# Loading batch 0 pair by pair, starting its products at unit 5, and turning its last 64 tokens in one group

## The chip, the cores and the metric

The kernel runs on one core of a Trainium2 chip. A core has five engines that run their own instruction streams side by side and wait for each other through semaphores: TensorE (matrix multiplications into PSUM), VectorE and ScalarE (elementwise work, evacuation of PSUM), GpSimd (here copies, and the issue of all loads that cast from fp32 to fp16) and SyncE (issue of stores and of transposes by DMA). Sixteen DMA engines move the data. The metric is the device time of one execution in microseconds, less is better.

## The reference: attention, then a gated feed-forward network

```python
# q, k, v: (8 batches, 12 heads, 448 tokens, 64), fp32
scores = (q @ k.transpose(0, 1, 3, 2)) / sqrt(64)
attn   = softmax(scores, axis=-1)
x      = (attn @ v).transpose(0, 2, 1, 3).reshape(8 * 448, 768)
# w_gate, w_val: (768, 1536), w_out: (1536, 768)
g   = x @ w_gate
out = (g * sigmoid(g) * (x @ w_val)) @ w_out      # (3584, 768), fp32
```

## The kernel before

Two heads make a pair; 6 pairs make a batch, 48 pairs in all. The 448 tokens of a head are taken as 4 chunks of 112. A unit is one chunk of keys of one pair: scores of both heads (two matmuls), one exponential on ScalarE over 112 x 896, and one piece of the product with the values (8 matmuls, summed in PSUM over the 4 chunks of the pair). Units 0 to 23 are batch 0; only after them does the feed-forward network have an input, X, which is kept transposed (features on partitions, two batches of tokens side by side in one tile). Blocks of feed-forward work alternate between 384 and 512 tokens: block 0 is tokens 0 to 383 of batch 0, block 1 is the rest of batch 0 and all of batch 1.

Queries and keys are turned by TensorE for pairs 0 to 10 and by DMA from pair 11 (`NPE`) on. The product of a pair, divided by its sums, is turned into X by TensorE for pairs 0 to 11 and by DMA from pair 12 (`XPE`) on.

```python
NPE = 11; LA = 6; RB = 5; FIRST = 6; WIDE = 8; XPE = 12
NE = 4; NX = 3; NV = 6; VS = 6      # buffers of E, xt, vo, and pairs in vraw

def load_qk16(pr, n=2):             # n pairs of q and of k, cast by the load
    ...
        nc.gpsimd.dma_start(dst[:, ds(h0, 2 * n)], flat...)

def load_v(pr, n=1):                # n pairs of values
    ...
def copy_v(pr):
    nc.vector.tensor_copy(Vts[pr % NV][:, :, :, 0:D], vraw[:, pr % VS])

    def turn():                     # in prep(pr): q and k of one pair
        ...
        for t in range(2):
            for c in range(NC):
                for hx in range(2):
                    src = raw[pr][t][:, hx, c, :]
                    nc.tensor.transpose(tp[ts(hx, 64), (1 - t) * NC + c, 0:P], src, ident[0:P, 0:P])
        nc.vector.tensor_copy(qkT[pr][:, 0 : 2 * S]..., tp[:, :, 0:P])
        nc.vector.tensor_copy(qkT[pr][:, 2 * S :], tp[:, NC, 0:D])

def qk(pr, c):                      # one unit: scores and exponential
    ...
    nc.scalar.activation(e[:, :, 0:S], s[0:P, :, 0:S], AF.Exp, scale=sm_scale)

def pv_chunk(pr, c):                # one piece; after the last one:
    ...
    nc.vector.reciprocal(r[:, 0:7], a7[:, :, D])
    nc.vector.tensor_tensor(xt..., a7[:, 0:n, 0:D], r..., ALU.mult)

def turn_x(pr):                     # into X: 3 x 128 tokens and a rest of 64
    ...
    if pr < XPE:
        for j in range(3):
            nc.tensor.matmul(tp[:, ds(D + 128 * j, 128)], lhsT=xt[:, j], rhs=ident[:], ...)
        for hx in range(2):
            nc.tensor.matmul(tp[ts(hx, D), 0:D], lhsT=xt[:, 3, 0:D], rhs=ident[:, ts(hx, D)], ...)
        nc.vector.tensor_copy(dst, tp[:, 0:S])
        return
    nc.sync.dma_start_transpose(dst[:, D:S]..., xt[:, 0:3]...)
    nc.sync.dma_start_transpose(dst[:, 0:D]..., xt[0:D, 3])

# ---- order of work at the start ----
load_qk32(0)                        # pair 0 in fp32, from SyncE
load_qk16(1, 1); load_qk16(2, 1); load_qk16(3, 1)
load_v(0, GP)                       # pairs 0 to 2 (GP = 3) in one transfer
load_qk16(4)                        # pairs 4 and 5
load_v(3, GP)
...
wq = {                              # more loads, when a pair is entered
    0: [("qk", 6), ("g", 0), ("v", 0)],
    1: [("qk", 8), ("g", 1), ("v", 1)],
    3: [("qk", 10), ("V", 2), ("g", 2), ("v", 2)],
    4: [("g", 3), ("v", 3), ("qk", 12)],
    6: [("V", 3), ("o", 0)],        # w_out, in two halves
    7: [("o", 1)],
}
for u in range(FIRST * NC):         # batch 0
    pr, c = divmod(u, NC)
    qk(pr, c)
    ...
    elif u >= 6 and c == 2:
        prep(pr + 2)()              # turn q and k of a later pair
    if u in (5, 6, 7):
        dummy(1)                    # a 512-column matmul on zeros
    if u in (6, 14):
        for p in range(3):
            copy_v(u // 8 * 3 + p)
    ...
    if u in XAT:
        turn_x(XAT.index(u))
    for _ in range(1 if c == 2 or u in XAT else 2):
        if u >= 8 and pieces[0][0] * NC + pieces[0][1] <= u - 3:
            piece()
# then visits of 2 or 3 units with feed-forward work between them;
# block 1 begins two visits after pair 11's product
```

Of the kernel before, what the change touches and what calls it, by code (L numbers as in the profile page):

```python
# [10 lines left out]
FP32 = mybir.dt.float32  # L11
FP16 = mybir.dt.float16
AF = mybir.ActivationFunctionType
ALU = mybir.AluOpType
# [4 lines left out]
GP = 3  # L19
# [3 lines left out]
FIRST = 6  # L23
WIDE = 8
XPE = 12
NE = 4
NX = 3
NV = 6
VS = 6
EB = 15  # L30


# [1 line left out]
def kernel(  # L34
# [21 lines left out]
    GPB = NHP // GP  # L56
    sm_scale = float(D) ** -0.5
    OH = DM // 2

    tabs = list(get_activation_tables(nc.m.arch).keys())  # L60

# [22 lines left out]
    Xts = [consts.tile([128, 4, 128], FP16, name=f"xt{i}") for i in range(NX)]  # L84
# [70 lines left out]
    def prep(pr):  # L155
        rq, rk = raw[pr]
        if pr == 0 or pr >= NPE:
            qk16 = attp.tile([P, 2, NC, 2, D], FP16, tag="qk16", bufs=3)
            for t, src in enumerate((rq, rk)):
                dst = qk16[:, 1 - t].rearrange("p c h d -> p h c d")  # L160
                if pr == 0:
                    nc.vector.tensor_copy(dst[:, 0], src[:, 0])
                    nc.scalar.activation(dst[:, 1], src[:, 1], AF.Copy)
                else:
                    nc.gpsimd.tensor_copy(dst, src)  # L165
        qkT[pr] = attp.tile([128, 2 * S + D], FP16, tag="qkT", name="qkT", bufs=5)
        if pr >= NPE:
            nc.sync.dma_start_transpose(
                qkT[pr][:, 0 : 2 * S].rearrange("p (c q) -> p c q", q=P),
                qk16[:].rearrange("p t c h d -> p (t c h d)"),  # L170
            )
            nc.sync.dma_start_transpose(
                qkT[pr][:, 2 * S :].rearrange("p (c q) -> p c q", c=1),
                qk16[0:D, 1, 0].rearrange("p h d -> p (h d)"),
            )
            return None

        def turn0():
            for t in range(2):
                tp = ps_s.tile([128, 2, 512], FP32, tag="s", name="tp")  # L180
                for c in range(NC):
                    for hx in range(2):
                        nc.tensor.matmul(
                            tp[ts(hx, 64), c // 2, ds(c % 2 * P, P)],
                            lhsT=qk16[:, 1 - t, c, hx],
                            rhs=ident[0:P, 0:P],
                            start=True,
                            stop=True,
                        )
                dst = qkT[pr][:, ts(1 - t, S)].rearrange("p (a x) -> p a x", a=2)  # L190
                nc.vector.tensor_copy(dst[:, 0], tp[:, 0, 0 : 2 * P])
                nc.scalar.activation(dst[:, 1], tp[:, 1, 0 : 2 * P], AF.Copy)
                if t == 0:
                    tq = tp
            nc.vector.tensor_copy(qkT[pr][:, 2 * S :], tq[:, 0, 0:D])  # L195

        def turn():
            if pr < FIRST + 2:
                tp = ps_s.tile([128, 2 * NC, 256], FP16, tag="s", name="tp")
            else:  # L200
                tp = ps_f.tile([128, 2 * NC, 128], FP16, tag="f", name="tp")
# [5 lines left out]
            nc.vector.tensor_copy(  # L207
                qkT[pr][:, 0 : 2 * S].rearrange("p (c q) -> p c q", q=P), tp[:, :, 0:P]
            )
            nc.vector.tensor_copy(qkT[pr][:, 2 * S :], tp[:, NC, 0:D])  # L210

        return turn if pr else turn0

# [22 lines left out]
    def pv_chunk(pr, c):  # L236
        if c == 0:
            accs[pr] = ps_f.tile([128, 512], FP32, tag="f", name="acc")
        e = Es[pr % NE]
        vo = Vts[pr % NV]  # L240
        a7 = accs[pr][:, 0 : 7 * (D + 1)].rearrange("p (s d) -> p s d", s=7)
        for j in range(3):
            for hx in range(2):
                nc.tensor.matmul(  # L244
                    a7[:, 2 * j + hx],
                    lhsT=e[:, ds(c * EB + 9 * hx + 2 * j, 2)].rearrange("p b x -> p (b x)"),
                    rhs=vo[:, hx, c, 0 : D + 1],
                    start=c + j + hx == 0,
                    stop=False,
                )  # L250
# [12 lines left out]
        n = 7 if pr < XPE else 6  # L263
        nc.vector.reciprocal(r[:, 0:7], a7[:, :, D])  # L264
        nc.vector.tensor_tensor(  # L265
            xt[:].rearrange("p j (h d) -> p (j h) d", h=2)[:, 0:n],
            a7[:, 0:n, 0:D],
            r[:, 0:n].unsqueeze(2).to_broadcast([128, n, D]),
            ALU.mult,
        )  # L270
# [11 lines left out]
    def turn_x(pr):  # L282
# [6 lines left out]
        if pr < XPE:  # L289
            tp = accs[pr] if pr < FIRST else ps_f.tile([128, 512], FP32, tag="f", name="xtp")  # L290
            for j in range(3):
                nc.tensor.matmul(
                    tp[:, ds(D + 128 * j, 128)], lhsT=xt[:, j], rhs=ident[:], start=True, stop=True
                )
            for hx in range(2):
                nc.tensor.matmul(
                    tp[ts(hx, D), 0:D],
                    lhsT=xt[:, 3, 0:D],
                    rhs=ident[:, ts(hx, D)],
                    start=True,  # L300
                    stop=True,
                )
            nc.vector.tensor_copy(dst, tp[:, 0:S])
            return
        nc.sync.dma_start_transpose(
            dst[:, D:S].rearrange("p (j q) -> p j q", j=3), xt[:, 0:3].rearrange("p j m -> p (j m)")
        )
        nc.sync.dma_start_transpose(dst[:, 0:D].rearrange("p (j q) -> p j q", j=1), xt[0:D, 3])

    gate_small = [False]  # L310

# [32 lines left out]
    def ffn2_steps(kk, c0, n, hts, first, last_block):  # L344
# [6 lines left out]
        for ch, oh in steps:  # L351
# [7 lines left out]
            for m0, w in parts:  # L359
# [15 lines left out]
                l = l0  # L375
                while l < l0 + 128:
                    b, j = divmod(l, S)
                    c, p0 = divmod(j, P)
                    m = min(P - p0, l0 + 128 - l)
                    eng = nc.scalar if last and m < 64 else nc.sync  # L380
                    eng.dma_start(
                        out[ts(NB * kk + b, S), :].rearrange("(p c) m -> c p m", c=NC)[
# [13 lines left out]
    with tc.manual_schedule():  # L396
# [77 lines left out]
        for u in range(FIRST * NC):  # L474
# [51 lines left out]
        for x, (chunks, todo) in enumerate(plan):  # L526
# [3 lines left out]
            if x == 0:  # L530
# [2 lines left out]
                    piece()  # L533
                turn_x(5)
                add_block(0, end)
            for p0 in vcopies.get(x, []):
                copy_v(p0)
            entered = [pr for pr, c in chunks if c == 0]
            for pr in entered:
                if NPE <= pr + 3 < NPAIR:  # L540
# [26 lines left out]
            else:  # L567
# [60 lines left out]
```

The softmax here doesn't subtract the row's maximum and nothing guards it: scores larger than these inputs give would overflow.

## Time and profile before

| | |
|---|---|
| device time, median of 3 | 454.37 us (453.79 to 454.4) |
| span of the profiled execution | 453.1 us |
| loads issued by GpSimd, share of 16 DMA engines over the span | 41.7% |
| stores and DMA transposes issued by SyncE, the same | 29.6% |
| a load of one pair's q, k or v: 112 KB, median from issue to landing | 3.9 to 4.5 us |
| a load of w_gate or w_val: 288 KB a half, the same | 11.2 to 11.5 us |
| a half of w_out: 1152 KB, the same | 22.6 us |

In the profile a line such as `27.70 4.33 ACT L226 ACTIVATE E<-s ... x5 [0.36 <-PE s L218]` reads: from 27.70 us on, 4.33 us long, ScalarE ran five activations of line 226 that write tile E from tile s; before them it stood idle for 0.36 us, until TensorE's line 218 released it. PE is TensorE, DVE VectorE, ACT ScalarE, POOL GpSimd, SPq SyncE's queue. Sizes of loads are those of the fp16 data that arrive.

### The profile page before, as it was taken

The page shows a single profiled execution, that of the slowest core. Times are in us where ns is not written, and L with a number is a line of the kernel's source. Part 1 is how long each engine was busy: PE and PEld are TensorE (multiplying, and loading weights), DVE is VectorE, ACT ScalarE, POOL GpSimd, SP SyncE. Part 2 cuts the span into 40 slices and gives each one's busy share as a digit, 9 for nine tenths or more (in the row PEclk, how much of TensorE's full clock was granted, in tenths as well). Part 3 has the DMA queues.
Part 4 walks back from the last instruction along what each step waited for, and adds up shares of the span by engine and source line. Part 5 has one row for each costly group of instructions (what it writes and reads, how often), then busy time and mean ns, then how long its engine had stood idle before and what let it go on. Part 6 is the DMA issues. An engine that isn't in the chain of part 4 may idle for free.

```text
span 453.1 us, 9845 instructions
## 1 busy us (share of the span) xinstructions
PE 443.6 (98%) x4007; PEld 247.1 (55%) x4007; DVE 201.3 (44%) x456; ACT 239.1 (53%) x350; POOL 138.0 (30%) x222
## 2 busy tenths in 40 slices
PE   8889999999999999999999999999999999999996
PEld 3555655645455656545456665545455656644464
DVE  3555653356563535354443553444354444145400
ACT  6874576766555555645556446644654644222222
POOL 8454715927453225252322504440100000000000
PEclk9999999999999999999999999999999999999999
DMA  8999999999787739983867837974323102110033
GB/s 131 192 199 201 182 179 166 176 213 139 99 106 109 84 79 148 135 102 80 138 62 118 129 72 119 148 87 84 73 41 78 46 12 80 49 34 1 0 106 104
DMA packets 104941, 48.71 MB, mean 108 GB/s; under 512 B 59584, under 2 KB 101440, under 8 KB 104896
## 3 DMA queue, kind: packets, MB, share of 16 engines
q0 software_dynamic: 43296, 23.37, 41.7%
q1 hardware_dynamic: 61504, 24.66, 29.6%
q8 instruction: 31, 0.51, 0.4%
q14 instruction: 14, 0.11, 0.1%
q10 hardware_dynamic: 96, 0.05, 0.0%
HBM read 47.19 MB, written 11.01 MB: 128 GB/s over the span
## 4 chain that ended last, share of the span: by engine, by line
PE 90%; DMA 4%; DVE 2%; ACT 2%; POOL 1%; issue 1%; DVEq 0%; ACTq 0%; POOLq 0%
PE op L362 24%; PE gp L317 23%; PE vp L317 23%; PE acc L244 8%; PE s L218 8%; DMA vraw<-in_v_dram 4%; PE acc L252 2%; ACT E L226 1%; PE tp L206 1%; DVE t L336 1%; POOL k L127 0%; ACT sg L332 0%; DVE qkT L207 0%; POOL q L127 0%; DVE vo L140 0%
## 5 line engine op out<-in xcount | busy, mean ns | idle before, releaser
L226 ACT ACTIVATE E<-s 112x896 f16<-112x896 f32 x192 | 162.6, 918 | 29.9 <-PE s L218 29.3
L317 PE MATMUL vp<-X,wv 128*128 128x384 f16 (+1 forms) x576 | 124.7, 353 | 0.4 <-DVE qkT L210 0.4
L317 PE MATMUL gp<-X,wg 128*128 128x384 f16 (+1 forms) x576 | 124.7, 352 | 0.0
L362 PE MATMUL op<-wo,hts 128*128 128x384 f16 (+1 forms) x684 | 116.0, 323 | 0.0
L336 DVE SCALAR_TENSOR_TENSOR t<-sg,gp 128x384 f32<-128x384 f32 (+1 forms) x96 | 59.6, 621 | 120.7 <-ACT sg L332 120.7
L332 ACT ACTIVATE sg<-gp 128x384 f32<-128x384 f32 (+1 forms) x96 | 52.4, 546 | 85.2 <-PE gp L317 84.0
L362 PEld LDWEIGHTS <-hts 128*128 128x128 f16 x684 | 65.5, 98 | 45.9 <-issue 3.9
L317 PEld LDWEIGHTS <-wv 128*128 128x128 f16 x576 | 56.3, 98 | 53.3 <-DVE qkT L210 0.8
L317 PEld LDWEIGHTS <-wg 128*128 128x128 f16 x576 | 53.1, 97 | 45.6 <-issue 1.1
L369 ACT ACTIVATE osb<-op 128x384 f32<-128x384 f32 (+1 forms) x57 | 27.7, 487 | 92.5 <-PE op L362 91.0
L339 DVE SCALAR_TENSOR_TENSOR hts<-t,vp 128x384 f16<-128x384 f32 (+1 forms) x96 | 59.6, 621 | 10.8 <-PE vp L317 0.5
L165 POOL COPY qk<-q 112x512 f16<-112x512 f16 x37 | 22.9, 619 | 129.2 <-DMA qkT<-qk 128.0
L244 PEld LDWEIGHTS <-E 112*128 112x128 f16 x1152 | 46.3, 97 | 19.1 <-issue 16.6
L244 PE MATMUL acc<-vo,E 112*128 112x65 f16 x1152 | 53.0, 193 | 2.3 <-DVE vo L140 1.3
L218 PE MATMUL s<-qkT 64*128 64x448 f16 x384 | 50.4, 353 | 0.6 <-DVE qkT L195 0.3
L252 PE MATMUL acc<-vo,E 112*128 112x65 f16 x384 | 42.9, 193 | 0.0
L264 DVE RECIPROCAL R<-acc 128x7 f32<-128x7 f32 x48 | 9.8, 205 | 73.8 <-PE acc L252 73.8
L134 POOL DMA_DIRECT2D vraw<-in_v_dram x40 | 26.7, 667 | 31.2 <-DVE vo L140 17.9
L127 POOL DMA_DIRECT2D k<-in_k_dram x42 | 27.8, 662 | 10.3 <-DMA wo<-in_moe_w_out_dram 7.2
L127 POOL DMA_DIRECT2D q<-in_q_dram x42 | 28.0, 667 | 4.2 <-PE tp L206 1.7
L218 PEld LDWEIGHTS <-qkT 64*128 64x128 f16 x384 | 14.6, 94 | 26.4 <-issue 19.6
L265 DVE TENSOR_TENSOR xt<-acc,R 128x384 f16<-128x384 f32 (+1 forms) x48 | 27.6, 575 | 1.7
(42 smaller groups left out, 150.6 us busy)
## 6 DMA issues: line engine op xcount, KB each, us to landing
q<-in_q_dram POOLq DMA_DIRECT2D x37, 112.0 KB, 3.9
k<-in_k_dram POOLq DMA_DIRECT2D x37, 112.0 KB, 4.4
vraw<-in_v_dram POOLq DMA_DIRECT2D x36, 112.0 KB, 4.5
out_dram<-osb SPq DMA_DIRECT2D x7, 336.0 KB, 3.3
wg<-in_moe_w_gate_dram POOLq DMA_DIRECT2D x8, 288.0 KB, 11.5
wv<-in_moe_w_val_dram POOLq DMA_DIRECT2D x8, 288.0 KB, 11.2
wo<-in_moe_w_out_dram POOLq DMA_DIRECT2D x2, 1152.0 KB, 22.6
out_dram<-osb SPq DMA_DIRECT2D x8, 288.0 KB, 3.3
```

Of the source, the lines that this page charges most:

```text
L127: nc.gpsimd.dma_start(dst[:, ds(h0, 2 * n)], flat.rearrange("h (p c) d -> p h (c d)", c=NC))
L218: nc.tensor.matmul(s[:, hx, 0:S], lhsT=t[ts(hx, 64), c * P : c * P + 128], rhs=t[ts(hx, 64), ds(S + (1 - hx) * D, S)], start=True, stop=True,)
L226: nc.scalar.activation(e[:, :, 0:S], s[0:P, :, 0:S], AF.Exp, scale=sm_scale)
L244: nc.tensor.matmul(a7[:, 2 * j + hx], lhsT=e[:, ds(c * EB + 9 * hx + 2 * j, 2)].rearrange("p b x -> p (b x)"), rhs=vo[:, hx, c, 0 : D + 1] ...
L252: nc.tensor.matmul(a7[:, 6], lhsT=e[:, ds(c * EB + 6 + hx, 2)].rearrange("p b x -> p (b x)"), rhs=vo[:, hx, c, 0 : D + 1], start=False, st ...
L265: nc.vector.tensor_tensor(xt[:].rearrange("p j (h d) -> p (j h) d", h=2)[:, 0:n], a7[:, 0:n, 0:D], r[:, 0:n].unsqueeze(2).to_broadcast([12 ...
L317: nc.tensor.matmul(dst[:, 0:n], lhsT=wslice(kind, fb, cb), rhs=X[kk][:, cb, ds(c0, n)], start=(cb == 0), stop=(cb == NCB - 1),)
L332: nc.scalar.activation(sg[:, 0:n], gp[:, 0:n], AF.Tanh, scale=0.5)
L336: nc.vector.scalar_tensor_tensor(t1[:, 0:n], sg[:, 0:n], 1.0, gp[:, 0:n], ALU.add, ALU.mult)
L339: nc.vector.scalar_tensor_tensor(hts[:, fb, 0:n], t1[:, 0:n], 0.5 * HS, vp[:, 0:n], ALU.mult, ALU.mult)
L362: nc.tensor.matmul(op[:, 0:w], lhsT=hts[:, fb, ts(ch, 128)], rhs=wo[oh][:, fb, ds(m0 - oh * OH, w)], start=(fb == 0), stop=(fb == NFB - 1),)
L369: nc.scalar.activation(osb[:, ds(m0, w)], op[:, 0:w], AF.Copy, scale=1.0 / HS)
```

## The change

Values of batch 0 are loaded pair by pair, each between the queries and keys of the pairs around it, and pairs 4 and 5 no longer come in one load. Product pieces may start at unit 5 in place of 8, spread over the units, and the three dummy matmuls at units 5 to 7 go. Values of pairs 6 to 8 are requested right behind the first weights, ahead of pair 8's queries and keys.

X puts the 64 rest tokens of each batch at the end of its 448 columns, not at the start. Block 0 needs the first 384 only, so the rests of batch 0 are turned together later, on TensorE, in `turn_rests`. For pairs 6 to 11 the rest is scaled into a tile of its own and turned by DMA, as it is from pair 12 on; their other 384 tokens stay with TensorE. The rows of the stores follow the new order of tokens. Turning queries and keys now writes the extra 64 columns by two more transposes, so that one copy evacuates all 960 columns.

```diff
-NX = 3
-NV = 6
-VS = 6
+NX = 6
+NV = 5
+VS = 9
...
-            for t in range(2):
-                for c in range(NC):
-                    for hx in range(2):
-                        src = raw[pr][t][:, hx, c, :]
-                        nc.tensor.transpose(tp[ts(hx, 64), (1 - t) * NC + c, 0:P], src, ident[0:P, 0:P])
-            nc.vector.tensor_copy(... 2 * S ...)
-            nc.vector.tensor_copy(qkT[pr][:, 2 * S :], tp[:, NC, 0:D])
+            for i in range(2 * NC + 1):
+                t, c = (1 - i // NC, i % NC) if i < 2 * NC else (0, 0)
+                for hx in range(2):
+                    src = raw[pr][t][:, hx, c, :]
+                    nc.tensor.transpose(tp[ts(hx, 64), ts(i, P)], src, ident[0:P, 0:P])
+            nc.vector.tensor_copy(qkT[pr][:], tp[:, 0 : 2 * S + D])
...
-        n = 7 if pr < XPE else 6
+        n = 7 if pr < FIRST else 6
...
-        if pr < XPE:
+        if pr < FIRST:
             return
         for hx in range(2):
             nc.vector.tensor_scalar(
-                xt[0:D, 3, ts(hx, D)], a7[ts(hx, D), 6, 0:D], r[ts(hx, D), 6:7], None, ALU.mult
+                Xrs[pr % 3][:, ts(hx, D)], a7[ts(hx, D), 6, 0:D], r[ts(hx, D), 6:7], None, ALU.mult
             )
...                                  # in turn_x, for pairs below XPE
-            for hx in range(2):
-                nc.tensor.matmul(tp[ts(hx, D), 0:D], lhsT=xt[:, 3, 0:D], ...)
-            nc.vector.tensor_copy(dst, tp[:, 0:S])
-            return
+            nc.vector.tensor_copy(dst[:, 0:MQ], tp[:, 0:MQ])     # MQ = 384
+            if pr < FIRST:
+                return
+        else:
+            nc.sync.dma_start_transpose(dst[:, 0:MQ]..., xt[:, 0:6]...)
+        nc.sync.dma_start_transpose(dst[:, MQ:S]..., Xrs[pr % 3][:])
+
+    def turn_rests():
+        tp = ps_f.tile([128, NHP, D], FP32, tag="f", name="rtp")
+        for p in range(FIRST):
+            for hx in range(2):
+                nc.tensor.matmul(tp[ts(hx, D), p], lhsT=Xts[p][:, 6], rhs=ident[:, ts(hx, D)], ...)
+        nc.vector.tensor_copy(X[0][:, :, MQ:S], tp[:])
...                                  # rows of the stores
-                    c, p0 = divmod(j, P)
-                    m = min(P - p0, l0 + 128 - l)
+                    c, p0 = divmod((j + D) % S, P)
+                    m = min(P - p0, l0 + 128 - l, (MQ if j < MQ else S) - j)
...
         load_qk16(2, 1)
+        load_v(0)
         load_qk16(3, 1)
-        load_v(0, GP)
-        load_qk16(4)
+        load_v(1)
+        load_qk16(4, 1)
+        load_v(2)
+        load_qk16(5, 1)
         load_v(3, GP)
...
-            1: [("qk", 8), ("g", 1), ("v", 1)],
-            3: [("qk", 10), ("V", 2), ("g", 2), ("v", 2)],
+            1: [("V", 2), ("qk", 8, 1), ("g", 1), ("v", 1)],
+            3: [("qk", 9, 1), ("qk", 10), ("g", 2), ("v", 2)],
...
-        XAT = (11, 15, 17, 20)
+        XAT = (11, 15, 17, 21)
+        CAT = (4, 7, 11, 14, 17, 21)
...
-            if u in (5, 6, 7):
-                dummy(1)
-            if u in (6, 14):
-                for p in range(3):
-                    copy_v(u // 8 * 3 + p)
+            if u in CAT:
+                copy_v(CAT.index(u))
...
-            for _ in range(1 if c == 2 or u in XAT else 2):
-                if u >= 8 and pieces[0][0] * NC + pieces[0][1] <= u - 3:
+            for _ in range(2 if c == 3 else int(c != 2 or u > 12)):
+                if u >= 5 and pieces[0][0] * NC + pieces[0][1] <= u - 3:
                     piece()
...                                  # in the visits: copies of values moved behind the work,
-            for p0 in vcopies.get(x, []):
-                copy_v(p0)
...
+            if x == 2:               # and the rests of batch 0
+                turn_rests()
+            for p0 in vcopies.get(x, []):
+                copy_v(p0)
```

More of the change, by code (lines that the diff above doesn't have):

```diff
@@ L58 @@
     OH = DM // 2
+    MQ = S - D
     tabs = list(get_activation_tables(nc.m.arch).keys())
@@ L83 @@
     Es = [consts.tile([P, NC * EB + 1, D], FP16, name=f"E{i}") for i in range(NE)]
-    Xts = [consts.tile([128, 4, 128], FP16, name=f"xt{i}") for i in range(NX)]
+    Xts = [consts.tile([128, 7, D], FP16, name=f"xt{i}") for i in range(NX)]
+    Xrs = [consts.tile([D, 128], FP16, name=f"xr{i}") for i in range(3)]
     Vts = [consts.tile([P, 2, NC, D + 2], FP16, name=f"vo{i}") for i in range(NV)]
@@ L198, in turn @@
             if pr < FIRST + 2:
-                tp = ps_s.tile([128, 2 * NC, 256], FP16, tag="s", name="tp")
+                tp = ps_s.tile([128, 2, 1024], FP16, tag="s", name="tp")[:, 0]
             else:
-                tp = ps_f.tile([128, 2 * NC, 128], FP16, tag="f", name="tp")
-            for t in range(2):
-                for c in range(NC):
-                    for hx in range(2):
-                        src = raw[pr][t][:, hx, c, :]
-                        nc.tensor.transpose(tp[ts(hx, 64), (1 - t) * NC + c, 0:P], src, ident[0:P, 0:P])
[L207 to L210, printed above, removed]
+                tp = ps_f.tile([128, 1024], FP16, tag="f", name="tp")
+            for i in range(2 * NC + 1):
[4 more added lines that the diff above has]
+            nc.vector.tensor_copy(qkT[pr][:], tp[:, 0 : 2 * S + D])
         return turn if pr else turn0
@@ L262, in pv_chunk @@
         xt = Xts[pr % NX]
-        n = 7 if pr < XPE else 6
         nc.vector.reciprocal(r[:, 0:7], a7[:, :, D])
+        n = 7 if pr < FIRST else 6
         nc.vector.tensor_tensor(
-            xt[:].rearrange("p j (h d) -> p (j h) d", h=2)[:, 0:n],
+            xt[:, 0:n],
             a7[:, 0:n, 0:D],
@@ L292, in turn_x @@
                 nc.tensor.matmul(
-                    tp[:, ds(D + 128 * j, 128)], lhsT=xt[:, j], rhs=ident[:], start=True, stop=True
-                )
+                    tp[:, ts(j, 128)],
+                    lhsT=xt[:, 2 * j : 2 * j + 2].rearrange("p h d -> p (h d)"),
+                    rhs=ident[:],
+                    start=True,
+                    stop=True,
+                )
+            nc.vector.tensor_copy(dst[:, 0:MQ], tp[:, 0:MQ])
+            if pr < FIRST:
+                return
+        else:
+            nc.sync.dma_start_transpose(
+                dst[:, 0:MQ].rearrange("p (j q) -> p j q", j=3),
+                xt[:, 0:6].rearrange("p j d -> p (j d)"),
+            )
+        nc.sync.dma_start_transpose(dst[:, MQ:S].rearrange("p (j q) -> p j q", j=1), Xrs[pr % 3][:])
+    def turn_rests():
+        tp = ps_f.tile([128, NHP, D], FP32, tag="f", name="rtp")
+        for p in range(FIRST):
             for hx in range(2):
                 nc.tensor.matmul(
-                    tp[ts(hx, D), 0:D],
-                    lhsT=xt[:, 3, 0:D],
+                    tp[ts(hx, D), p],
+                    lhsT=Xts[p][:, 6],
                     rhs=ident[:, ts(hx, D)],
@@ L302, in turn_x @@
                 )
-            nc.vector.tensor_copy(dst, tp[:, 0:S])
-            return
[L305 to L308, printed above, removed]
+        nc.vector.tensor_copy(X[0][:, :, MQ:S], tp[:])
     gate_small = [False]
```

## The prediction

> **What bounds the kernel now.** I read the page first (shares, slices, chain), then the timelines of TensorE and ScalarE up to 65 us, then those of GpSimd and SyncE from 57 to 96 us, then single DMA issues with their time to landing.
>
> The page, parts 1 and 2:
>
> ```profile
> PE 443.6 (98%) x4007; PEld 247.1 (55%) x4007; DVE 201.3 (44%) x456; ACT 239.1 (53%) x350; POOL 138.0 (30%) x222
> PE   8889999999999999999999999999999999999996
> ACT  6874576766555555645556446644654644222222
> DMA  8999999999787739983867837974323102110033
> ```
>
> TensorE is busy 98% of the span; from the fourth slice on (33 us) it is at nine tenths or more up to the last slice, and its whole list of waits adds up to under 6 us. What can be gained lies before 33 us, where batch 0's attention runs without feed-forward work to fill gaps. But the DMA row is at eight or nine tenths through the first eleven slices (125 us) too. Loads there follow their own clock, and TensorE, moved forward, may run into it.
>
> ScalarE in that first stage (columns: start, busy time, instruction, idle time before it and who ended it):
>
> ```profile
> 6.27 7.51 ACT L226 ACTIVATE E<-s 112x896 f16<-112x896 f32 x9 [0.25 <-PE s L218]
> 14.89 1.80 ACT L226 ACTIVATE E<-s 112x896 f16<-112x896 f32 x2 [1.11 <-PE s L218]
> 27.70 4.33 ACT L226 ACTIVATE E<-s 112x896 f16<-112x896 f32 x5 [0.36 <-PE s L218]
> ```
>
> TensorE at the start of the feed-forward work and at a later wait:
>
> ```profile
> 33.05 1.15 PE L317 MATMUL gp<-X,wg 128*128 128x384 f16 x6
> 39.65 1.15 PE L317 MATMUL vp<-X,wv 128*128 128x384 f16 x6 [0.44 <-DVE qkT L210]
> ```
>
> Nine exponentials take 7.51, so 0.834 us each back to back. The 26 that precede the first feed-forward matmul could end at 6.27 + 26 x 0.834 = 27.95; they end at 32.03. The hole of 1.11 is the wait for the values of pairs 0 to 2, one 336 KB transfer issued at 5.86 that lands 7.7 later, at 13.56. After it TensorE has to catch up on products at 0.88 to 1.16 us a unit and ScalarE waits for it. The feed-forward work starts at 33.05.
>
> Now the far end of the loading stage, first GpSimd:
>
> ```profile
> 65.00 0.65 POOL L127 DMA_DIRECT2D k<-in_k_dram  x1 [7.20 <-DMA wo<-in_moe_w_out_dram]
> 73.36 0.66 POOL L134 DMA_DIRECT2D vraw<-in_v_dram  x1 [7.71 <-DMA wo<-in_moe_w_out_dram]
> 80.10 0.62 POOL L165 COPY qk<-q 112x512 f16<-112x512 f16 x1
> 80.65 0.62 POOL L165 COPY qk<-k 112x512 f16<-112x512 f16 x1
> ```
>
> SyncE in the same time:
>
> ```profile
> 81.30 1.25 SPq L168 DMA_TRANSPOSE qkT<-qk  x1
> 82.59 1.23 SPq L172 DMA_TRANSPOSE qkT<-qk  x1
> 83.93 1.01 SPq L381 DMA_DIRECT2D out_dram<-osb  x2
> 85.04 1.25 SPq L305 DMA_TRANSPOSE X<-xt  x1
> ```
>
> TensorE at the start of block 1 (tokens 384 to 895):
>
> ```profile
> 89.42 1.46 PE L317 MATMUL gp<-X,wg 128*128 128x512 f16 x6
> ```
>
> And what the transposes issued at 85.04 and at 86.39 took from issue to landing (last column, us):
>
> ```profile
> X<-xt SPq DMA_TRANSPOSE x1, 7.6
> X<-xt SPq DMA_TRANSPOSE x1, 6.6
> ```
>
> GpSimd stands still until the second half of w_out has landed (issued at about 46.6, 26.2 to landing, so 72.8), then works without a gap. Its copies for pair 16 end at 81.25, and SyncE, which issues in program order at 1.2 us per transpose, sends pair 16's two transposes at 81.30 and 82.59. None of this waits for TensorE.
>
> [...] Here six 384-column matmuls follow each other every 0.97 us in the feed-forward part, so I take it as really full. [...] in the unloaded part, a transpose of X lands 2.3 us after issue, and at 85 us 6.6 to 7.6. [...]
>
> **The change part by part.**
>
> *Values pair by pair, products from unit 5.* The value load of pair 0 becomes 112 KB and takes the place in the queue that pair 3's queries have now, which land at 4.57 + 4.5 = 9.1. Its copy and the first product piece at unit 5 (scores at 9.7 today) no longer wait. Cost of units 5 to 23 on TensorE, by steps read between starts in the old trace: scores and one piece 0.65 (25.15 to 25.80), with two pieces 0.88 (18.56 to 19.45), with transposes and one piece 1.16, here 1.22 for 18 instead of 16 transposes; without a piece 0.87; a turn of X adds 0.27 (its two rest matmuls, 0.15, are gone). The new order has 8 units of 0.65, 2 of 0.88, 2 of 1.15, 2 of 0.92, 2 of 0.87, 3 of 1.22: 16.5 us. From 9.7 that gives unit 24 at 26.2 (29.68 now); ScalarE needs 6.27 + 22 x 0.834 = 24.6 to free the score buffer, so it no longer limits. From unit 24 to the first feed-forward matmul it takes 3.37 now, less 2 x 0.15: start at 29.3. **Gain 3.8 us.** The three dummy matmuls taken out sit in this slack and are in it.
>
> *Values of pairs 6 to 8 earlier.* They land at 38.65 now, and VectorE's wait passes 0.44 to TensorE at 39.65. Requested right behind the first weights they come some 10 us sooner. **Gain 0.4.**
>
> *Rest tokens.* For pairs 6 to 11 two matmuls of a rest (0.15 per pair, 0.9) leave TensorE; batch 0's twelve come back in one group, by the same price at most 0.9, by overlap of column halves perhaps 0.6. Three pairs get two transposes more (0.2). **About 0.1 gained.** One copy of 960 in place of 0.62 and 0.18 helps VectorE, which is not the bound.
>
> Sum of what TensorE gains up to block 1: 3.8 + 0.4 + 0.1 = **4.3 us**.
>
> *What turns DMA.* The rest of pairs 6 to 11 is now two scalings on VectorE (0.28 each) and one transpose on SyncE instead of two matmuls. Block 1 reads all six strips, pair 11's in the sixth matmul of its first group. The new order of SyncE puts this transpose behind pair 16's two transposes and two output stores, and pair 10's, also new, between pairs 14 and 15. So: pair 14's transposes stay at 75.2 and 76.5, pair 10's rest takes 1.2 behind them, pair 15's start at 79.0 (78.25 now) and end at 81.5; pair 16's go at 81.55 and 82.8 (81.30 and 82.59 now), the stores at 84.1, and pair 11's rest at 85.2. Landing in the same traffic, 6.2 to 6.6 later (the store issued at 83.95 took 6.2, the small transpose at 86.4 took 6.6): **91.6**. The old kernel comes to this sixth matmul at 89.42 + 5 x 0.216 = 90.5; the new one would be there at 86.2, and waits 5.4. It leaves this place **1.1 us later** than the old kernel: all 4.3 are given back and more.
>
> Is the loads' clock itself moved? Bytes before the end of w_out are the same. There are four transposes of rests more (some 0.1 us each, as a share of what a pair's transposes take from the loads in 50 to 66), and the small loads of the first 15 us are less efficient: today's move some 130 GB/s up to 12 us and 200 later. I take **0.3 later** in all, give or take 0.8.
>
> *The end.* The last two stores were 112 rows on SyncE and 16 on ScalarE's queue side by side; now two of 64 rows, both on SyncE: one issue of 0.32 more, **0.3**. After block 1 nothing else on TensorE changes.
>
> Sum: 454.4 + 1.1 + 0.3 + 0.3 = 456.1.
>
> **Rivals.** (1) *The gain stays.* If pair 11's rest lands by 86, all 4.3 arrive at the end: 450.4. For it: the strip is only 16 KB, and a loaded queue may let it pass sooner than the 98 KB transposes around it. Against: it is issued only when GpSimd's chain from 73.36 lets it, whatever its own size; even a landing in 3 us gives 88.2, and a gain of 2.3 less 0.6: 452.7. (2) *Earlier loads gate instead.* Pair 13's transposed queries and keys land at 73.3 and are used at 78.6; pair 14's at 82.3 and 87.8; w_out's first half at 64.5 and 71.1. Margins of 5.3, 5.5 and 6.6 against 4.3 hold, barely; a delay of 2 us in the loads would stop TensorE there, but the stop at block 1 hides these, and the time would be 457 to 458. (3) *The first stage gains less.* VectorE's copies in order, or a value load late, may keep the start at 31. If block 1's wait is what I think, that alone changes nothing at the end: it only makes the wait shorter.
>
> **Range and chances.** The wait gives a narrow bundle from 455 to 458, to which I give some two thirds; the rest lies mostly below, between 450.5 and 455, for a landing sooner than thought. Weighing it, I put the centre a little under the sum: **455.8 us, 451.5 to 458.5**. Two percent are 9.1 us; neither way reaches that: faster 0.02, same 0.95, slower 0.03.
>
> **What would show it.** Feed-forward start at 29 to 30; ScalarE's hole at 13.8 gone; no wait at about 35 for a value copy; GpSimd's first value load after w_out still near 73.4; then a wait of some 5 us on TensorE in block 1's first gate group, ended by a DMA into X. Wrong, if that group starts near 85 and runs through, or if the first gate group of block 0 starts after 31.

## The result and the profile after

The changed kernel takes 470.64 us (median of 4 runs, 469.62 to 471.75), the kernel before, run beside it, 454.38 us (4 runs, 453.79 to 455.12). The ratio is 1.0357, with a 95% interval of 1.0326 to 1.0389: slower by 3.6%, 16.3 us. The prediction was 455.8 us with a range of 451.5 to 458.5, and 0.95 on "within 2%". It is wrong.

The page of the kernel after, parts 1 and 2:

```profile
PE 445.4 (95%) x4012; PEld 247.8 (53%) x4012; DVE 204.7 (44%) x458; ACT 239.2 (51%) x350; POOL 141.5 (30%) x228
...
PE   8998899689899999999999999999999999999995
...
ACT  6965657444646456743655465564554643222121
...
PEclk9999999889999999999999999999999999999998
DMA  9999999997675739766674847963423102110033
```

TensorE's busy time has hardly changed (443.6 before, 445.4 now), but its share has fallen from 98% to 95%: 15 of the 17 us that the span grew by (453.1 to 470.0) are idle. Only one slice shows a large part of this, the eighth (82 to 94 us) with its 6. A slice is 11.75 us long, and its digit reads 9 for anything from 90% up, so a loss of 2 or 3% in every later slice is not seen in this row. The clock row has 8s at the eighth and ninth slices, where the kernel before has 9s.

What TensorE waited for says more. The list of waits of the kernel after (us in all, times, longest):

```profile
PE acc L243 <- DVE vo L142: 12.5, 22, 1.6
PE gp L328 <- DMA X<-xr: 3.8, 1, 3.8
```

The second line is the stop that the prediction is about. The first is not in it at all: 22 times a product of attention (acc) stands still until VectorE has copied the pair's values (vo). The kernel before had this wait once, for 1.3 us.

TensorE at block 1 in the kernel after; the line of the kernel before at 89.42 answers to the one at 87.89:

```profile
87.89 1.24 PE L328 MATMUL gp<-X,wg 128*128 128x512 f16 x5
92.95 0.59 PE L328 MATMUL gp<-X,wg 128*128 128x512 f16 x1 [3.81 <-DMA X<-xr]
93.33 2.76 PE L328 MATMUL vp<-X,wv 128*128 128x512 f16 x6
95.89 2.74 PE L328 MATMUL gp<-X,wg 128*128 128x512 f16 x6
98.45 1.47 PE L328 MATMUL vp<-X,wv 128*128 128x512 f16 x6
99.86 0.74 PE L217 MATMUL s<-qkT 64*128 64x448 f16 x6
```

Five matmuls of the gate group run, the sixth waits for the DMA into X, and then two groups of six take 2.75 us each where such a group takes 1.46 at the end of this list.

To see where the time goes, I took the same five places in the profiles of several kernels and subtracted the kernel before (us; negative is earlier). The last evacuation of the kernel before, on ScalarE, is

```profile
449.59 0.33 ACT L369 ACTIVATE osb<-op 128x192 f32<-128x192 f32 x1 [0.56 <-PE op L362]
```

and that of the kernel after, at 464.74, is shown under e4. The labels are those of the experiments below.

| place (kernel before) | after | e1 | e3 | e4 | e6 | e7 |
|---|---|---|---|---|---|---|
| feed-forward work starts (33.05) | -3.41 | -3.66 | -2.97 | -3.06 | -3.10 | -3.62 |
| first gate group of block 1 starts (89.42) | -1.53 | -4.03 | -0.69 | -2.65 | -1.58 | -3.80 |
| scores that follow its first four groups (94.69) | +5.17 | +4.74 | -0.69 | -2.65 | +2.10 | -3.79 |
| last evacuation starts (449.59) | +15.15 | +4.75 | +8.80 | -2.64 | +12.03 | -3.61 |
| end of the span (453.1) | +16.9 | +6.5 | +10.4 | -1.0 | +13.8 | -3.1 |

The column "after" reads: 3.4 gained at the start; 1.9 of it lost again by block 1; 6.7 lost there; 10.0 lost between block 1 and the last evacuation; 1.75 lost behind it.

How the copies bring TensorE to a halt is seen in one visit. VectorE in the kernel after:

```profile
103.37 0.69 DVE L347 SCALAR_TENSOR_TENSOR t<-sg,gp 128x512 f32<-128x512 f32 x1 [2.60 <-ACT sg L343]
104.16 0.69 DVE L350 SCALAR_TENSOR_TENSOR hts<-t,vp 128x512 f16<-128x512 f32 x1
104.77 0.71 DVE L142 COPY vo<-vraw 112x512 f16<-112x512 f16 x1
```

and TensorE in the same kernel, just behind it:

```profile
105.53 0.34 PE L243 MATMUL acc<-vo,E 112*128 112x65 f16 x6 [1.57 <-DVE vo L142]
```

In this trace VectorE does its work in the order of the program. The copy now stands behind the visit's feed-forward work, whose first operation had to wait 2.60 us for ScalarE's sigmoid (102.73 to 103.34), and that reads what TensorE's own matmuls had written by 102.00. The values had long been there (pair 14's load was issued at 80.02 and landed 6.0 later, 18.7 us before the copy); only the place in the queue was late. In the kernel before the copy of the same visit stood ahead of that work. VectorE there:

```profile
95.53 0.29 DVE L140 COPY vo<-vraw 112x512 f16<-112x512 f16 x1
98.21 0.69 DVE L336 SCALAR_TENSOR_TENSOR t<-sg,gp 128x512 f32<-128x512 f32 x1 [2.39 <-ACT sg L332]
99.00 0.69 DVE L339 SCALAR_TENSOR_TENSOR hts<-t,vp 128x512 f16<-128x512 f32 x1
```

The copy falls into VectorE's idle time before the sigmoid and is done about 3 us before TensorE's product, which begins with no wait. TensorE in the kernel before:

```profile
98.95 0.34 PE L244 MATMUL acc<-vo,E 112*128 112x65 f16 x6
```

### The profile page after: what moved, and what is told of

Its sections match the earlier page's. It is cut to its first block, busy times and chain, and to the rows that moved or that the text cites. A ratio compares the mean times of both kernels' runs of the same rounds, so it can differ in the third digit from the quotient of the medians.

```text
span 470.0 us, 9866 instructions
## 1 busy us (share of the span) xinstructions
PE 445.4 (95%) x4012; PEld 247.8 (53%) x4012; DVE 204.7 (44%) x458; ACT 239.2 (51%) x350; POOL 141.5 (30%) x228
## 4 chain that ended last, share of the span: by engine, by line
PE 84%; DVE 8%; ACT 4%; DMA 1%; issue 1%; DVEq 0%; ACTq 0%
PE op L373 23%; PE gp L328 23%; PE vp L328 18%; PE acc L243 9%; PE s L217 6%; DVE t L347 3%; DVE hts L350 3%; ACT sg L343 3%; PE acc L251 2%; ACT E L225 2%; DVE vo L142 1%; DMA X<-xr 1%; PE tp L208 1%; PE wp L109 1%; PE acc L291 0%
## 5 line engine op out<-in xcount | busy, mean ns | idle before, releaser
L328 PE MATMUL gp<-X,wg 128*128 128x384 f16 (+1 forms) x576 | 126.4, 355 | 3.8 <-DMA X<-xr 3.8
L328 PE MATMUL vp<-X,wv 128*128 128x384 f16 (+1 forms) x576 | 126.0, 355 | 0.0
L243 PEld LDWEIGHTS <-E 112*128 112x128 f16 x1152 | 47.4, 97 | 29.6 <-issue 24.1
L129 POOL DMA_DIRECT2D k<-in_k_dram x44 | 28.9, 657 | 9.3 <-DMA wo<-in_moe_w_out_dram 8.0
L129 POOL DMA_DIRECT2D q<-in_q_dram x44 | 29.2, 664 | 4.6 <-PE s L217 1.8
L136 POOL DMA_DIRECT2D vraw<-in_v_dram x42 | 27.9, 663 | 8.5 <-DMA X<-xr 7.6
```

Source lines behind the costliest of these rows:

```text
L129: nc.gpsimd.dma_start(dst[:, ds(h0, 2 * n)], flat.rearrange("h (p c) d -> p h (c d)", c=NC))
L136: nc.gpsimd.dma_start(vraw[:, ds(pr % VS, n)].rearrange("p r h c d -> p (r h) (c d)"), v[b, h : h + 2 * n].rearrange("h (p c) d -> p h (c ...
L243: nc.tensor.matmul(a7[:, 2 * j + hx], lhsT=e[:, ds(c * EB + 9 * hx + 2 * j, 2)].rearrange("p b x -> p (b x)"), rhs=vo[:, hx, c, 0 : D + 1] ...
L328: nc.tensor.matmul(dst[:, 0:n], lhsT=wslice(kind, fb, cb), rhs=X[kk][:, cb, ds(c0, n)], start=(cb == 0), stop=(cb == NCB - 1),)
```

## The experiments

Theory A: the copies of values behind the visits' work cost the 10 us after block 1 (and most of the 1.9 before it); the DMA that turns pair 11's rest makes the stop at block 1; the stores make the loss at the end. Theory B: the stop and its slow clock are the cause, and the waits for copies are only where a shifted TensorE happens to wait.

### e1: the change, with the copies back in their old place

```diff
+            for p0 in vcopies.get(x, []):     # ahead of the visit's work, as before
+                copy_v(p0)
             entered = [...]
             ...
-            for p0 in vcopies.get(x, []):     # behind it, as changed
-                copy_v(p0)
```

> The changed kernel with the value copies put back ahead of a visit's feed-forward work; nothing else undone. Theory (late copies): in the changed kernel TensorE stands 14.2 us after block 1's start (9.3 before matmuls, 4.9 before weight loads) for VectorE's copy of values, which now stands behind the last gate product of the visit. Taking that away should give back about 12 us: 458 to 460, with the wait for a DMA into X at block 1 kept, or longer by the 2.6 us of copies' waits that lay ahead of it. Rival (the stop at block 1 and the halved clock after it are the loss, the copies only fill slack): 467 or more.

Measured: 460.59 us (460.23 to 461.34), against 454.51 for the kernel before on the same chip: 1.0123 (1.0087 to 1.0159). That is 10.05 us less than the changed kernel, where I had expected about 12 (458 to 460). TensorE's waits in e1:

```profile
PE gp L328 <- DMA X<-xr: 7.3, 1, 7.3
...
PE acc L243 <- DVE vo L142: 0.6, 1, 0.6
```

The waits for copies are gone, and in the table the shift is +4.74 behind block 1 and +4.75 at the last evacuation: nothing more is lost between. The stop at block 1 has grown, since TensorE comes there earlier (TensorE in e1):

```profile
93.93 0.59 PE L328 MATMUL gp<-X,wg 128*128 128x512 f16 x1 [7.30 <-DMA X<-xr]
94.31 2.60 PE L328 MATMUL vp<-X,wv 128*128 128x512 f16 x6
96.75 1.46 PE L328 MATMUL gp<-X,wg 128*128 128x512 f16 x6
```

This is the kernel that the prediction had described: 4.0 us gained up to block 1, then a stop that gives back more.

### e2: the kernel before, with only the copies moved

```diff
-            for p0 in vcopies.get(x, []):
-                copy_v(p0)
             entered = [...]
             ...
+            for p0 in vcopies.get(x, []):
+                copy_v(p0)
```

> The kernel before with nothing changed but the value copies moved behind a visit's feed-forward work. Theory (late copies): it loses what the changed kernel loses by them, 2.6 us ahead of block 1 and some 12 after it, so 466 to 470. Rival (only together with the stop at block 1): within 2 us of 454.4.

Measured: 465.4 us (465.24 to 466.39), 1.0231 (1.0195 to 1.0268). This one move costs 10.9 us with nothing else changed, a little less than expected (466 to 470); e2 has no transposed rest and no stop at block 1, and its granted clock is 1.0 over the span. Theory B falls. TensorE's waits in e2:

```profile
PE acc L244 <- DVE vo L140: 11.8, 19, 1.3
```

### e3: the change, with the rests of pairs 6 to 11 back on TensorE

```diff
-        n = 7 if pr < FIRST else 6
+        n = 7 if pr < XPE else 6
...
-        if pr < FIRST:
+        if pr < XPE:
             return
...                                   # in turn_x, pairs 6 to 11
-            nc.vector.tensor_copy(dst[:, 0:MQ], tp[:, 0:MQ])
+            for hx in range(2):
+                nc.tensor.matmul(tp[ts(hx, D), MQ:S], lhsT=xt[:, 6], rhs=ident[:, ts(hx, D)], ...)
+            nc.vector.tensor_copy(dst, tp[:, 0:S])
```

> The changed kernel with the rests of pairs 6 to 11 turned by TensorE again, as two matmuls each (0.15 us a pair), copies left late. Theory (stop at block 1): the wait of 3.8 us and the halved clock behind it go; the sixth matmul of block 1's first group ran at 92.95 and could run at about 89.0, and the stretch from it to the next scores took 6.9 us in place of 4.2: 4.0 + 2.7 - 0.9 for the matmuls = 5.8 us, so 464 to 466. Rival (the rests by DMA cost nothing, since the copies' waits would take the place of this one): 469 or more.

In this form, and in e4, the rest of pair 6 is written over that of pair 0 before batch 0's group is turned, so 64 tokens of pair 0 carry pair 6's values; e8 below gives these rests a tile of their own. Measured: 465.95 us (464.93 to 467.05), 1.0239 (1.0198 to 1.028), 4.7 less than the changed kernel. TensorE at block 1 in e3:

```profile
88.73 1.46 PE L334 MATMUL gp<-X,wg 128*128 128x512 f16 x6
...
94.00 0.74 PE L217 MATMUL s<-qkT 64*128 64x448 f16 x6
```

No stop, no slow group: -0.69 goes into the four groups and -0.69 comes out. Behind them the late copies take 9.5 (to +8.80).

### e4: both undone

> Both undone: copies ahead of the work and rests of pairs 6 to 11 on TensorE; what is left of the change is the start (values pair by pair, pieces from unit 5, pairs 6 to 8 earlier, batch 0's rests in one group). Theory: the 3.4 us by which the feed-forward work starts sooner (29.64 against 33.05) and some 0.5 at the value copy reach the end, less 0.3 for the stores: 450 to 451.5. Rival (another wait on loads takes the gain, since loads keep their own clock): 453.5 or more.

The edits of e1 and e3 together. Measured: 453.51 us (453.35 to 454.9, 20 runs), 0.9978 (0.9967 to 0.9988). Both together are worth 17.1 us. Taken one by one they are not additive: copies first 10.05 and then the rests 7.08, or rests first 4.69 and then the copies 12.44, because copies that hold TensorE up before block 1 shorten the stop there (3.8 us with late copies, 7.3 in e1).

I had expected 450 to 451.5, and this was missed. The number is the rival's (453.5 or more), but its cause is not seen: no wait of TensorE for a load stands in e4's list. The gain of 2.64 is whole at the last evacuation, but only 1.0 reaches the end of the span. The tail of the kernel after, whose stores e4 shares, on ScalarE:

```profile
464.74 0.33 ACT L380 ACTIVATE osb<-op 128x192 f32<-128x192 f32 x1 [0.61 <-PE op L373]
```

and on SyncE:

```profile
464.53 2.47 SPq L392 DMA_DIRECT2D out_dram<-osb  x4
```

The last store is issued at 467.0, 2.3 us after the last evacuation began, because SyncE takes some 0.6 us for each store of 64 rows and four are still to come. In the kernel before, ScalarE issued the store of 16 rows itself (ScalarE's queue there):

```profile
449.95 0.38 ACTq L381 DMA_DIRECT2D out_dram<-osb  x1
```

and SyncE was done at 450.26, 0.7 after its last evacuation began. In `nc.scalar if last and m < 64`, the condition no longer holds for the last stores of the new order, which are two of 64 rows.

### e8: the rests of pairs 6 to 11 in a tile of their own

```diff
+    Xqs = [consts.tile([128, D], FP16, name=f"xq{i}") for i in range(3)]
...                                   # at the end of pv_chunk, pairs 6 to 11
+            nc.vector.tensor_scalar(Xqs[pr % 3][:], a7[:, 6, 0:D], r[:, 6:7], None, ALU.mult)
...                                   # in turn_x
-                ... lhsT=xt[:, 6], rhs=ident[:, ts(hx, D)] ...
+                ... lhsT=Xqs[pr % 3][:], rhs=ident[:, ts(hx, D)] ...
```

> As the kernel with both undone, but with a tile of its own for the rests of pairs 6 to 11 (there, pair 6's rest took the place of pair 0's before that was turned); one scaling more on VectorE for each of six pairs. Theory: it costs TensorE nothing, 453.0 to 454.2, the time of the kernel with both undone. Rival: VectorE's extra scalings delay it by 0.1 us a pair, 454.2 to 455.

e4 with the overwriting taken out. Measured: 453.44 us (22 runs), 0.9981 (0.9974 to 0.9989). Nothing was lost by it, so what e4 shows does not hang on the overwritten rest.

### e5: e8, with half of the last stores issued by ScalarE

```diff
-                    eng = nc.scalar if last and m < 64 else nc.sync
+                    eng = nc.scalar if last and p0 == 0 else nc.sync
```

> The former with one thing more: of the last two stores of each part (64 rows each) the second is issued by ScalarE, as the shorter one was in the kernel before. Theory (stores pile up on SyncE): with both undone the last 64-row issue begins 1.34 us after the last evacuation ends, in the kernel before 0.03; from the last evacuation to the end of the span it takes some 1.6 us longer. So 1.3 to 1.6 us less than the former: 451.6 to 452.6. Rival (0.3 us, as predicted): within 0.4 us of the former.

Measured: 452.53 us (12 runs), 0.9963 (0.9952 to 0.9973), 0.9 less than e8. The stores at the end do cost time, but less than the 1.3 to 1.6 that I had put on them: from the start of the last evacuation to the end of the span it is 5.1 us in e8, 4.0 in e5 and 3.5 in the kernel before. What makes the last 0.5 is open.

### e7: e5, with batch 0's rests turned later

```diff
-            if x == 2:
+            if x == 9:
                 turn_rests()
```

> The former with the rests of batch 0 turned seven visits later, in a visit without a product, where TensorE does output projections. Theory: where they stand now they cost 0.92 us, 0.38 for twelve matmuls and 0.54 for the PSUM tile that pair 6's turn then waits for; later only the 0.4 stays: 0.4 to 0.6 us less than the former. Rival (the wait moves with them): no difference.

In the changed kernel the group of twelve rests stands between the feed-forward groups, and what follows waits for VectorE. TensorE in the kernel after:

```profile
42.92 0.38 PE L312 MATMUL rtp<-ident,xt 128*64 128x64 f16 x12
43.84 0.33 PE L291 MATMUL xtp<-ident,xt 128*128 128x128 f16 x3 [0.54 <-DVE hts L350]
```

Moved to a later visit, the wait of 0.5 is gone. Measured: 452.32 us (451.76 to 454.08, 6 runs), 0.9954 (0.9939 to 0.997): 0.2 less than e5 by the medians, within what the runs of e5 spread by, and below the 0.4 to 0.6 expected. As a step by itself it is inconclusive by the times; in the profiles the stretch from the first feed-forward matmul to block 1 takes 56.2 us in e7 and 56.8 in e5, so 0.6 is gained there. As a whole e7 is faster than both kernels, the fastest of this study together with e10. Its shift is -3.80 at block 1 and -3.61 at the last evacuation: the gain at the start comes through when nothing takes it back.

### e11: e7, with the values of pairs 6 to 8 requested late again

```diff
-            1: [("V", 2), ("qk", 8, 1), ("g", 1), ("v", 1)],
-            3: [("qk", 9, 1), ("qk", 10), ("g", 2), ("v", 2)],
+            1: [("qk", 8, 1), ("g", 1), ("v", 1)],
+            3: [("qk", 9, 1), ("qk", 10), ("V", 2), ("g", 2), ("v", 2)],
```

> The former, but with the values of pairs 6 to 8 requested again where the kernel before has them (behind pairs 10 and 11). Theory: they land near 38.6, as in the kernel before, while their copy now stands at about 34, and VectorE waits for them in order, so the gain of the start is lost at this wait: 3 us or more above the former. Rival (as I predicted, the early request is worth the old wait of 0.44): 0.3 to 0.6 us above.

Measured: 457.14 us (455.05 to 460.03, 7 runs), 1.0055 (1.003 to 1.0079), 4.8 above e7. VectorE in e11:

```profile
39.15 0.29 DVE L143 COPY vo<-vraw 112x512 f16<-112x512 f16 x1 [4.64 <-DMA vraw<-in_v_dram]
```

TensorE in e11:

```profile
40.06 1.75 PE L338 MATMUL vp<-X,wv 128*128 128x384 f16 x6 [4.22 <-DVE qkT L210]
```

An evacuation of queries and keys stands behind the copy on VectorE, and TensorE waits for that. In the kernel before, this load landed at nearly the same time (38.65) and cost 0.44. A TensorE that runs 3.4 us ahead pays for it with all it had gained, and more: behind the stop the clock is at half for 3.4 us (the last section), which is 1.7 us of work. The one run of e11 with a granted clock of 1.0 took 455.05. So the earlier request, which by itself could save 0.4, is what lets the early start be kept.

### e6: the change, with 17 matmuls on zeros during the stop

```diff
+                    if (kk, c0, fb, kind, cb) == (0, 384, 0, "g", NCB - 1):
+                        dummy(17)      # 512 columns each, ahead of the sixth gate matmul
```

> The changed kernel with 17 matmuls on zeros (3.6 us at 0.213 each) put ahead of the sixth matmul of block 1's first gate group, to fill the wait for pair 11's rest. Theory (the clock is halved because TensorE stands idle there): the stretch from the end of the wait to the next scores falls from 6.9 us to about 4.2, the granted clock stays at 1.0, and the time falls by 2 to 2.7 us against the changed kernel's 470.6: 467.8 to 468.8. Rival (the clock falls for another reason, or the wait alone counts): 470 or more.

Measured: 468.83 us (468.1 to 469.39), 1.032 (1.0304 to 1.0336), 1.8 less than the changed kernel, just above what was expected (467.8 to 468.8). TensorE in e6:

```profile
88.92 3.83 PE L109 MATMUL wp<-warm 128*128 128x512 f16 x17
92.59 0.38 PE L330 MATMUL gp<-X,wg 128*128 128x512 f16 x1
92.81 1.46 PE L330 MATMUL vp<-X,wv 128*128 128x512 f16 x6
94.10 1.46 PE L330 MATMUL gp<-X,wg 128*128 128x512 f16 x6
```

The sixth matmul comes hardly sooner (92.59, 92.95 without the dummies), but the groups behind it take 1.46 again: the stretch from it to the next scores shrinks from 6.91 to 4.20 us. 2.7 us of the loss at block 1 in the profiled execution are the clock, not the wait. The medians differ by 1.8 only, and the profiled executions by 3.1. The clock does not fall alike in every execution of the changed kernel: its mean over the span was 0.990 in the profiled one (471.75 us), 0.996 and 0.993 in two others and 1.0 in the fastest (469.62 us), where 6.8 us at half would have made it 0.993. In e6 it was 0.997 to 0.999.

### e10: e7, with product pieces from unit 8 again

```diff
-            for _ in range(2 if c == 3 else int(c != 2 or u > 12)):
-                if u >= 5 and pieces[0][0] * NC + pieces[0][1] <= u - 3:
+            for _ in range(1 if c == 2 or u in XAT else 2):
+                if u >= 8 and pieces[0][0] * NC + pieces[0][1] <= u - 3:
```

> The best kernel so far (copies ahead, rests of pairs 6 to 11 on TensorE, last stores shared, batch 0's rests later) with the product pieces taken from unit 8 on again by the old rule, two a unit; loads and copies stay pair by pair. Theory (TensorE's even spread of pieces counts beside the values' landing): the feed-forward work starts 0.8 to 1.3 us later than that kernel's 29.4, 452.9 to 453.9 in all. Rival (the earlier values alone make the gain): 452 to 452.6, a start at 29.4 to 29.8.

Measured: 452.37 us (451.92 to 452.52, 5 runs), 0.9956 (0.9942 to 0.9969): the same as e7, and the rival's number. From the first exponential to the first feed-forward matmul it takes 23.3 us (6.85 to 30.16), in e7 23.1 (6.33 to 29.43), in the kernel before 26.8 (6.27 to 33.05). So the gain of the first stage hardly needs the pieces from unit 5 on: they are worth some 0.2 us there. What is left (loads and copies of values pair by pair, one evacuation for queries and keys, the dummy matmuls gone) was not tried one by one; that the values make the gain is argued from the wait for them that is gone.

## Why the prediction was wrong, point by point

**The failed step** is one sentence of "The end": "After block 1 nothing else on TensorE changes." The diff shows the copies of values moved behind the visit's work, in its last hunk, and no step of the prediction puts a cost on it. The move adds no instruction and leaves TensorE's stream as it was, so nothing shows there; the copy's place on VectorE had to be read against VectorE's idle time. Measured: 10.0 us between the scores behind block 1 and the last evacuation in the changed kernel, 0.0 with the copies back (e1), 10.9 in all when the old kernel gets this one edit (e2). Without it the changed kernel takes 460.6, which is still above the range: the terms of the stop and of the end were too small as well, as is shown below.

**Values pair by pair.** Right: 3.8 foreseen, 3.4 measured. TensorE starts its feed-forward work at 29.64 (kernel after):

```profile
29.64 1.14 PE L328 MATMUL gp<-X,wg 128*128 128x384 f16 x6
```

and ScalarE's hole of 1.11 us is gone there:

```profile
6.54 5.03 ACT L225 ACTIVATE E<-s 112x896 f16<-112x896 f32 x6 [0.33 <-PE s L217]
11.77 8.38 ACT L225 ACTIVATE E<-s 112x896 f16<-112x896 f32 x10 [0.20 <-PE s L217]
```

But my sum credited two edits together, and e10 reaches nearly the same start without one of them. That its size came out so close is in part luck.

**Values of pairs 6 to 8.** The wait of 0.44 is gone, as foreseen, but this was too narrow a view: at the new pace the edit guards some 4.8 us (e11).

**Rest tokens.** "About 0.1 gained". The twelve matmuls take 0.38, less than the 0.6 to 0.9 allowed (in the kernel before the two of one pair, 217 ns each, take 0.22 together); the wait of 0.54 behind them was not in the sum. Up to block 1, e1 gains 4.03, where the sum said 4.3.

**What turns DMA.** The mechanism was right, and e3 confirms it: with the rests on TensorE the stop is gone. SyncE in the kernel after issued the transpose of pair 11's rest at 87.29:

```profile
83.86 1.66 SPq L174 DMA_TRANSPOSE qkT<-qk  x1
85.61 1.58 SPq L392 DMA_DIRECT2D out_dram<-osb  x2
87.29 1.17 SPq L306 DMA_TRANSPOSE X<-xr  x1
```

and its time to landing in the list of DMA issues is

```profile
X<-xr SPq DMA_TRANSPOSE x1, 5.6
```

It was foreseen at 85.2 with 6.4 to landing, so 91.6; it is 87.29 + 5.6 = 92.9, and the sixth matmul, which reads this strip, starts at 92.95. SyncE came to pair 16's first transpose at 82.56, 1.0 later than foreseen, and then took 1.0 more to issue the second one and the two stores (1.66 and 1.58 where the old trace had 1.23 and 1.01). TensorE leaves this place 2.45 later than the old kernel, not 1.1. The wait is 3.81 instead of 5.4 because late copies had already delayed TensorE by 2.5 us (-1.53 at block 1, against -4.03 in e1); with them back in place it is 7.3 (e1), ending at 93.93 where 91.6 was foreseen, so 2.3 too late. **What follows the stop was missing from the sum**: the clock at half rate, 2.7 us in the profiled execution of the changed kernel, 1.3 in that of e1.

**The loads' clock.** "0.3 later": 0.4 later in the changed kernel, but 0.8 earlier in e1 (72.54), so no steady shift shows. GpSimd in the kernel after issues its first value load behind w_out at 73.78 (73.36 before):

```profile
73.78 0.65 POOL L136 DMA_DIRECT2D vraw<-in_v_dram  x1 [7.59 <-DMA X<-xr]
```

**The end.** "One issue of 0.32 more, 0.3": a size that was off. From the start of the last evacuation to the end of the span it is 5.26 (470.0 - 464.74) in place of 3.51, so 1.75. I counted one more store where a row of 64-row stores piles up on SyncE; e5 shows 0.9 of it.

**A reading.** The DMA row of the kernel before is at eight or nine tenths through ten slices (113 us), not eleven; nothing hangs on it.

**The rivals.** The first (the gain stays, 450.4) is what e7 comes near to, at 452.32, but only after its repairs; the changed kernel is far from it. The second (earlier loads gate) was not seen in the changed kernel, but e11 shows it at work as soon as one load is late again. The chance of 0.03 for "slower" rested on the claim that neither way reaches 9 us. That was a bound on the ways I had listed, not on the diff.

## What to carry to other kernels

When a diff moves an instruction without adding one, find it in its engine's queue and ask what stands ahead of it now and who needs its result: a 0.3 us copy behind work that waits for TensorE's own output stopped TensorE about twenty times, for 10 us. A bound that is busy 98% of the time has no slack to swallow such a wait, and no digit of its row shows it; its list of waits does. And where work moved forward meets a transfer that keeps its own clock, add to the wait what comes behind it, the clock above all (2.7 of the 6.7 us lost at block 1 here), and check every load that used to be just in time.

## What the runs showed of the hardware that was not expected

In three profiles TensorE's granted clock fell to half: during the stop of 3.8 us in the kernel after and that of 7.3 in e1, and just behind that of 4.2 in e11. It stayed there for 6.8, 6.8 and 3.4 us. Stretches of 0.4 us in the kernel after (length; busy time of TensorE, its weight loads, VectorE, ScalarE and GpSimd with counts; granted clock; DMA share; GB/s):

```profile
91.60:92.00 0.40, 0.00 (x0) 0.00 (x0) 0.00 (x0) 0.00 (x0) 0.40 (x2) 0.55 1.11 275
...
98.40:98.80 0.40, 0.40 (x3) 0.21 (x2) 0.00 (x0) 0.14 (x1) 0.00 (x0) 0.92 1.26 246
```

and in e1, whose stop is 7.3 us long:

```profile
89.40:89.80 0.40, 0.00 (x0) 0.00 (x0) 0.00 (x0) 0.00 (x0) 0.40 (x2) 0.98 2.65 88
...
96.40:96.80 0.40, 0.40 (x3) 0.20 (x2) 0.00 (x0) 0.00 (x0) 0.00 (x0) 0.74 1.15 352
```

Between these stretches the clock reads 0.50, before and after them 1.00. If it is taken to be at full or at half rate and nothing between, a mean of 0.55 over 0.4 us puts the fall at 91.64 (0.04 us at full rate, the rest at half); in the same way the return is at 98.46, and in e1 the two are at 89.78 and 96.61. Both times the clock is at half for 6.8 us; TensorE had stood still for 2.5 and 3.2 us when it fell, and had worked for 5.5 and 2.7 us when it came back. In e11, whose stop ends at 40.06, it is half as long:

```profile
40.20:40.60 0.40, 0.40 (x3) 0.19 (x2) 0.27 (x1) 0.00 (x0) 0.00 (x0) 0.80 1.33 204
...
43.80:44.20 0.40, 0.40 (x15) 0.40 (x13) 0.00 (x0) 0.32 (x1) 0.20 (x1) 0.93 1.24 192
```

By the same working the clock falls at 40.44, when TensorE has been at work again for 0.4 us, and returns at 43.86, after 3.4 us. In the 3.4 us ahead of the falls TensorE had been at work for 0.9 us (kernel after), 0.3 (e1) and 0.4 (e11). When the clock in the kernel after had been at half for 3.4 us, after which it was back in e11, TensorE had worked for 2.1 of them, and the clock stayed at half for 3.4 more. What decides when the clock falls and when it returns was not shown.

The same kind of stop cost 2.7 us of slow matmuls in the kernel after and 1.3 in e1: of the 6.8 us at half TensorE worked for 5.5 in the one and for 2.7 in the other, and half of that is lost: groups of six follow each other every 2.56 us there, every 1.30 at the full rate (e6). Why the mean clock in the changed kernel's fastest run is 1.0 was not shown. With matmuls on zeros through the stop (e6) the granted clock reads 1.00 in each 4 us from 88 to 100, and its mean over the span is 0.999, in the changed kernel 0.990.

A store of 64 rows took longer to issue than one of 16: 0.50 us from ScalarE in e7, 0.38 in the kernel before, and about 0.6 from SyncE in the tail of the kernel after. And the same copy of values on VectorE, 0.29 us as a rule, took 0.71 at 104.77, while GpSimd was running its own copy from 104.72 on; the 48 copies add up to 16.7 us in the kernel after, 14.5 before. GpSimd's copy alone does not decide it: in the kernel before, seven copies of values overlap with a copy on GpSimd, and four of these took 0.29. What slows it was not tried.
